# Totals of squares one half step later, and the products of w3 and w_out one step later, in a fused attention and expert kernel

## Chip, cores, metric

The kernel runs on one core of a Trainium2 chip. The metric is the device time of one execution in microseconds (us). The engines are named as in the profile: PE is TensorE (matmuls; PEld are its weight loads), DVE is VectorE, ACT is ScalarE, POOL is GpSimd, SP issues most DMAs.

## What is computed

```python
scores = np.where(mask, scale * np.matmul(q, k.transpose(0, 1, 3, 2)), -1000000000.0)
attn = softmax(scores)                 # 8 batches x 8 heads, 576 tokens, block mask of 64
x = np.matmul(attn, v)                 # put together to 4608 tokens x 512
h = (x @ w1) * (x @ w2) @ w3           # 512 -> 1024 -> 1024
x2 = h @ w_out                         # 1024 -> 512
logits = x2 @ w_gate                   # 8 experts, 576 tokens each, greedily by the largest logits
out[mask] = np.maximum(x2[mask] @ ew1[e], 0.0) @ ew2[e]
```

## The kernel before

Precise products are made from 16-bit halves: an array is scaled by a power of two, its high half is rounded to float16 by ACT (line 189), its low half is the rest, made by DVE (line 184), and a product is three matmuls (high x high, high x low, low x high). The power of two is found from a **total**: ACT squares the array and sums each row (line 203), PE sums over the 128 rows with one small matmul against a matrix of ones (`total`, line 146), and three or four short DVE instructions make the scale (`pow2`, lines 78 to 81).

The first part, up to some 700 us, interleaves three streams by an order that is written out with positions. `at(p, f)` puts a function at position p, `defer(d, f)` at d behind the present one, and functions run in the order of their positions; the unit is a **step**, about 8.5 us of PE without its extra pieces. PE issues exactly in this order. ACT, DVE and SP get their order from a scheduler that follows dependences and priorities, held by `issue_after` where `behind` is used. In step h PE does:

- the score matmuls (S, lines 330 and 394) of two tiles of rows: the second tile of half-pair h - 1 and the first of half-pair h. Eight half-pairs (steps) make one batch; group g of q and k (two head pairs of `GROUPS`) is first needed in step 8 (g // 2) + 2 (g % 2), so g = 6 in step 24, 7 in 26, 8 in 32 and so on to 15 in 58. From the fourth group on S takes the halves `qkT`: q high x k high, q high x k low, q low x k high, in this order;
- two units of the first feed-forward product (`moe_unit`, line 466, 24 matmuls each), at h + .26 and h + .60. Each takes two of the three slots of the PSUM pool `ps_ab`; ACT frees nothing before its copy `a_sb` (line 476), DVE's `g` (line 482) frees the second;
- the product of probabilities and v (PV, line 433) of an earlier half-pair, at h + .93. Behind it come ACT's and DVE's halves `xT` (lines 444 and 439).

In between ACT makes the exponentials E (line 356) and the high halves of P (line 372), DVE the maxima `nb` (line 348) and the low halves of P (line 376).

`qk_scale` prepares a group: two squares (`junk`), the total `qm`, and in `fin` two `split`s, q first, then k. A `split` asks `spread` for a place of its high half. `spread` knows two places for it in each step, .07 (behind `xT`) and .42 (behind the newest exponential, "e"); of the first two that are not before the present position and less than .75 behind it, it takes the one that fewer others have taken:

```python
PLACES = {"a": ((.07, "x"), (.42, "e")), "g": ((.3, "m"), (.58, "g")), ...
places = [x for x in places[:2] if x[0] < p + .75] or places[:1]
x, k = min(places, key=lambda x: taken_.get((key, round(x[0], 2)), 0))
```

Beside this, w_out and the eight column blocks f of w3 are read, decoded and split in the same way (`w3_chunk`, total `w3m`), and `w34` (lines 725 and 738) multiplies each block with w_out and with the gate, 24 + 16 matmuls. After the last `w34` the pool `es_g` is closed, `late_open` starts to load `g` back, and `late_run` makes the logits of eight units at a time (line 520). The second part (700 to 1024 us) multiplies with w3 w_out while DVE routes the tokens; the third does the experts.

Of the kernel before, what the change touches and what calls it, by code (L numbers as in the profile page):

```python
# [55 lines left out]
def moe_kernel(ctx, tc, q, k, v, moe_w1, moe_w2, moe_w3, moe_w_out, w_gate, ew1, ew2, out):  # L56
# [18 lines left out]
    def pow2(pool, m, name, TB=TB, **kw):  # L75
        n = m.shape[-1]
        t = pool.tile([P, 3, n], I32, name=name, **kw)
        nc.vector.tensor_scalar(t[:, 0], m.bitcast(I32), 24, 23, op0=ALU.logical_shift_right,
                                op1=ALU.logical_shift_left)
        nc.vector.tensor_scalar(t[:, 1], t[:, 0], -1.0, float((189 + TB) << 23), op0=ALU.mult, op1=ALU.add)  # L80
        nc.vector.tensor_scalar(t[:, 2], t[:, 0], float((65 - TB) << 23), None, op0=ALU.add)
        return t[:, 1].bitcast(F32), t[:, 2].bitcast(F32)
# [31 lines left out]
    ev, now, held = [], [-1.0], set()  # L114

    def at(p, f, *a):
        assert p >= now[0], (p, now[0])
        heapq.heappush(ev, (p, at.n, f, a))
        at.n += 1
# [3 lines left out]
    def defer(d, f, *a):  # L123
        at(now[0] + d, f, *a)
# [40 lines left out]
    def spread(key, p, f, *a, soon=False):  # L165
        p = max(p, now[0])
        if p < HS + .3:
            at(p, f, *a)
            return p
        if key == "a" and p > 2 * NS + 1:  # L170
            key = "t"
        places = [(x + y, k) for x in range(int(p), int(p) + 3) for y, k in PLACES[key]]
        places = [x for x in places if x[0] >= p - 1e-6]
        if soon:
            places = places[:1]
        places = [x for x in places[:2] if x[0] < p + .75] or places[:1]
        x, k = min(places, key=lambda x: taken_.get((key, round(x[0], 2)), 0))
        taken_[key, round(x, 2)] = taken_.get((key, round(x, 2)), 0) + 1
        at(x, behind, k, f, *a)
        return x  # L180

    def split(hi, lo, x, s, d=.1, p=0, then=None, key="g"):
        def low_half():
            nc.vector.scalar_tensor_tensor(lo, x, s, hi, op0=ALU.mult, op1=ALU.subtract)
            if then:
                then()

        def high_half():
            nc.scalar.activation(hi, x, AF.Copy, scale=s)
            if now[0] < HS + .3:  # L190
                defer(d, low_half)
            else:
                spread(key, now[0] + .1, low_half, soon=key != "g")

        spread("a", p, high_half, soon=key != "g")
# [5 lines left out]
    def ssq(x, dst, junk):  # L201
        with nc.allow_low_precision(reason='the sums only choose powers of two'):
            nc.scalar.activation(junk, x, AF.Square, accum_out=dst)

    def load_qk(g):
        n0, n1 = GROUPS[g]
        t = ld.tile([P, 2, 2, S], F32, name="qk32", bufs=2)
        step_ = 1 if g == 0 else 2
        for n in range(n0, n1, step_):
            for z, src in enumerate((q, k)):  # L210
                nc.sync.dma_start(t[:, z, n - n0:n - n0 + step_], src[n:n + step_].rearrange("n p s -> p n s"))
        qk32[g] = t
        if g < GF:
            for n in range(n0, n1):
                qkT[n] = t[:, 0, n - n0:n - n0 + 1], t[:, 1, n - n0:n - n0 + 1], q4f[:, n % 2:n % 2 + 1], c8
# [47 lines left out]
    pq = {}  # L263
# [3 lines left out]
    def qk_scale(g, d0, d1, d2):  # L267
        n0, n1 = GROUPS[g]
        w = n1 - n0

        def sq(z):
            if z == 0:
                pq[g] = sm.tile([P, 2], BF16, name="qm")
            ssq(qk32[g][:, z, :w], pq[g][:, z:z + 1], junk)
            if z:
                defer(d1 + (.45 if g > 5 else 0), total, pq[g], .08, fin)

        def fin(m2):
            T = c2.tile([P, 2, 2, 2, S], F16, name="qkT")
            s, e = pow2(sm, m2, "qp")  # L280
            c = sm.tile([P, 2], F32, name="cc")
            for z, f in enumerate((1.0, -1.0)):
                nc.vector.scalar_tensor_tensor(c[:, z:z + 1], e[:, 0:1], f * 0.125, e[:, 1:2],
                                               op0=ALU.mult, op1=ALU.mult)
            for z in range(2):
                split(T[:, z, 0, :w], T[:, z, 1, :w], qk32[g][:, z, :w], s[:, z:z + 1], .14,
                      then=lambda: end(d2), key="g5" if g == 4 else "g")
            pq[g] = s, c, T

        done = []  # L290

        def end(_):
            done.append(1)
            if len(done) < 2:
                return
            s, c, T = pq.pop(g)
            del qk32[g]
            for n in range(n0, n1):
                qkT[n] = T[:, 0, :, n - n0], T[:, 1, :, n - n0], q4[:, n % 2], c
            if g + 2 < len(GROUPS):  # L300
                load_qk(g + 2)

        if g == 4:
            defer(0, behind, "e", sq, 0)
            defer(.02, behind, "e", sq, 1)
            return
        spread("a", now[0], sq, 0)
        spread("a", now[0] + d0, sq, 1)

# [261 lines left out]
    def decode(key, dst, then):  # L571
        src = raw.pop(key)
        t = src.rearrange("p (n t) -> p n t", t=2)
        lo, hi = t[:, :, 0], t[:, :, 1]
        a = stg_w.tile([P, 1024], F32, name="dec2", bufs=1) if key[0] == "w" else stg.tile([P, 512], F32, name="dec", bufs=1)
        nc.scalar.activation(a, hi.bitcast(F32), AF.Abs)
        ai, d = a.bitcast(I32), dst.bitcast(I32)

        def clamp():
            nc.vector.tensor_scalar(a, a, HIMIN, HIMAX, op0=ALU.max, op1=ALU.min)  # L580
            nc.vector.tensor_scalar(ai, ai, 3, 0x3FFFFFF8, op0=ALU.logical_shift_left, op1=ALU.bitwise_and)

        def join():
            nc.vector.scalar_tensor_tensor(ai, lo, 29, ai, op0=ALU.logical_shift_right, op1=ALU.bitwise_or)
            nc.vector.scalar_tensor_tensor(d, hi, -(1 << 30), ai, op0=ALU.bitwise_and, op1=ALU.bitwise_or)
            next_load()
            defer(.05, then)

        defer(.1, clamp)
        defer(.2, join)  # L590
# [31 lines left out]
    wo = {}  # L622
# [75 lines left out]
    def w3_chunk(f, h):  # L698
        if h == 0:
            wo["w3"] = wo["p3"].tile([P, 1024], F32, name="w3d", bufs=1)  # L700
        w3 = wo["w3"]

        def use(m2):
            t = wo["T", f]
            s, e = pow2(sm, m2, "w3p")
            split(t[:, 0], t[:, 1], w3, s, .12, then=lambda: wo.update({("ok", f): True}))
            fc = sm.tile([P, 2], F32, name="w3f")
            nc.vector.tensor_tensor(out=fc[:, 0:1], in0=e, in1=wo["e"], op=ALU.mult)
            nc.vector.tensor_tensor(out=fc[:, 1:2], in0=e, in1=wo["ee"], op=ALU.mult)
            wo["T", f] = t.rearrange("p z (k f) -> p z k f", f=P), fc  # L710

        def squares():
            m = sm.tile([P, 1], BF16, name="w3m")
            wo["T", f] = wo["p3"].tile([P, 2, 1024], F16, name="w3h", bufs=2)
            at(spread("a", now[0], ssq, w3, m, wo["T", f][:, 1]) + .55, total, m, .06, use)

        decode(("3", f, h), w3[:, h * 512:h * 512 + 512], squares if h else lambda: None)

# [108 lines left out]
    for f in range(8):  # L827
        at(2 + .7 * f, prep_w, f)
        at(16.2 + .75 * f, wo_chunk, f)
        at(22.6 + .25 * f, wo_half, f)  # L830
        at(26.2 + .5 * f, wo_turn, f)
        at(29.6 + 3.2 * f, w3_chunk, f, 0)
        at(30.6 + 3.2 * f, w3_chunk, f, 1)
        at(int(33.28 + 3.2 * f) + .42, w34, f)
    at(22.2, wo_split)
    at(30.8, wo_gate)
    at(55.97, late_open)
    for h in range(UL // 8):
        at(57 + .87 * h, alone, "l", late_run, h)

    MS = {mybir.EngineType.PE}
    run(HS - .02)
# [538 lines left out]
    with tc.manual_schedule(engines={mybir.EngineType.PE, mybir.EngineType.Activation, mybir.EngineType.DVE}):  # L1381
# [3 lines left out]
        for p_ in range(E // 2):  # L1385
# [4 lines left out]
            a, b_, c = (0, 3, 6) if e == 0 else (3, 5, 8)  # L1390
# [44 lines left out]
```

## Time and profile before

| | us |
|---|---|
| median of three runs (range) | 1427.79 (1426.8 to 1428.41) |
| the profiled execution | 1425.24 |
| its span, first to last instruction | 1423.5 |
| mean granted clock of PE, share of full speed | 0.971 |
| PE busy, whole span | 1305.5 (92%) |
| DVE busy | 963.0 (68%) |
| ACT busy | 952.5 (67%) |

Busy time is time in which an engine ran an instruction; the rest is idle, and the views say what ended an idle stretch. The 1.7 us between the span and the execution's time lie around the first and last instruction.

### The profile page before, as it was taken

What the parts mean: (1) busy time and instruction counts of PE and PEld (TensorE: products, weight loads), DVE (VectorE), ACT (ScalarE), POOL (GpSimd) and SP (SyncE); (2) the same over time, 40 slices, a digit from 0 to 9 for tenths busy, and PEclk for the clock granted to TensorE, in tenths of its full rate; (3) what the DMA queues carried; (4) which work ended last, traced back from release to release, by engine and by line L of the source; (5) the groups of instructions that cost most, each with busy time, mean ns of one, the idle gap of its engine ahead of it and who ended that gap; (6) DMA issues with size and microseconds to landing.
All of it is one profiled execution on the core that took longest, in us unless ns stands there. A gap on an engine that the chain in (4) does not pass through costs nothing. (4 is left out here: it accounts for less than half of the span.)

```text
span 1423.5 us, 31849 instructions
## 1 busy us (share of the span) xinstructions
PE 1305.5 (92%) x12427; PEld 897.5 (63%) x12427; DVE 963.0 (68%) x2873; ACT 952.5 (67%) x2229; POOL 114.6 (8%) x141
## 2 busy tenths in 40 slices
PE   4669889888999989999999899999799999999997
PEld 2446567666766767666776566666586566655663
DVE  7989888887988878787415587877455456454530
ACT  7897887969888787876542555555247667675641
POOL 0000000000000000010010111101122221120001
PEclk9699999999999999999999899999989999999999
DMA  9887977797878768699999878988576677654201
GB/s 291 202 182 205 214 170 162 160 206 182 197 187 190 167 176 168 141 232 234 231 289 262 188 186 210 205 216 192 150 147 161 159 196 161 161 172 140 82 23 37
DMA packets 383814, 257.45 MB, mean 181 GB/s; under 512 B 260784, under 2 KB 344752, under 8 KB 382640
## 3 DMA queue, kind: packets, MB, share of 16 engines
q1 hardware_dynamic: 370464, 213.44, 61.6%
q0 software_dynamic: 11520, 39.87, 12.5%
q10 hardware_dynamic: 1680, 2.11, 0.5%
q8 instruction: 97, 1.59, 0.5%
q14 instruction: 53, 0.43, 0.1%
HBM read 130.84 MB, written 39.86 MB: 120 GB/s over the span
## 5 line engine op out<-in xcount | busy, mean ns | idle before, releaser
L466 PE MATMUL ab<-xT,w1h 128*128 128x288 f16 x1536 | 215.4, 289 | 12.3 <-DVE xT L439 4.0
L466 PE MATMUL ab<-xT,w2h 128*128 128x288 f16 x1536 | 212.2, 288 | 4.4 <-ACT a_sb L476 2.9
L1346 PE MATMUL pe<-xT,ewa 128*128 128x288 f16 (+2 forms) x1728 | 192.1, 274 | 1.6 <-ACT xT L1314 0.9
L466 PEld LDWEIGHTS <-w1h 128*128 128x128 f16 x1536 | 145.4, 99 | 68.8 <-issue 27.6
L1364 PE MATMUL pe<-ewb,h 128*128 128x512 f16 (+1 forms) x960 | 188.5, 379 | 0.0
L466 PEld LDWEIGHTS <-w2h 128*128 128x128 f16 x1536 | 150.8, 99 | 46.5 <-issue 6.9
L1346 PEld LDWEIGHTS <-ewa 128*128 128x128 f16 x1728 | 157.0, 99 | 36.3 <-issue 2.0
L376 DVE SCALAR_TENSOR_TENSOR P<-E,rr,P 128x128 f16<-128x128 f32 (+4 forms) x288 | 157.4, 584 | 23.7 <-ACT P L372 23.2
L356 ACT ACTIVATE E<-S,nb,cc 128x384 f32<-128x384 f32 (+4 forms) x234 | 148.0, 642 | 1.9
L1364 PEld LDWEIGHTS <-h 128*128 128x128 f16 (+1 forms) x960 | 84.7, 100 | 99.8 <-issue 2.6
L372 ACT ACTIVATE P<-E,rr 128x384 f16<-128x384 f32 (+2 forms) x224 | 120.7, 605 | 16.3 <-DVE rr L361 5.7
L1155 PE MATMUL px<-W34h,gl 128*128 128x512 f32 x288 | 120.1, 417 | 3.3 <-DMA gl<-g 3.3
L1155 PE MATMUL px<-W34h,gh 128*128 128x512 f32 x288 | 120.6, 419 | 2.3 <-ACT gh L1176 2.3
L1155 PE MATMUL px<-W34l,gh 128*128 128x512 f32 x288 | 120.0, 417 | 0.0
L433 PE MATMUL PV<-PT,v 128*64 128x128 f16 (+1 forms) x2880 | 89.9, 219 | 20.9 <-DMA PT<-P 19.7
L433 PEld LDWEIGHTS <-v 128*64 128x64 f16 x2880 | 79.0, 116 | 40.9 <-issue 32.2
L348 DVE TENSOR_REDUCE nb<-S 128x2 f32<-128x768 f32 (+3 forms) x128 | 100.7, 818 | 4.6 <-PE S L334 4.2
L1349 DVE SCALAR_TENSOR_TENSOR h<-pe,h 128x288 f16<-128x288 f32 (+2 forms) x144 | 57.8, 420 | 45.9 <-ACT h L1348 45.0
L1367 ACT ACTIVATE y<-pe,s 128x512 f32<-128x512 f32 x36 | 24.7, 687 | 94.8 <-PE pe L1364 59.6
L1304 DVE SCALAR_TENSOR_TENSOR x<-xg,xsc,x 128x512 f16<-128x512 f32 x36 | 27.1, 752 | 84.0 <-ACT x L1303 84.0
L1348 ACT ACTIVATE h<-pe 128x288 f16<-128x288 f32 (+2 forms) x144 | 52.6, 377 | 43.5 <-PE pe L1346 36.8
L1173 ACT ACTIVATE gl<-g 128x1024 fp32r<-128x1024 f32 x36 | 37.9, 1056 | 60.0 <-DMA g<-gd 59.9
(294 smaller groups left out, 2236.3 us busy)
## 6 DMA issues: line engine op xcount, KB each, us to landing
g<-gd SPq DMA_DIRECT2D x36, 512.0 KB, 5.3
gl<-g POOLq DMA_DIRECT2D x36, 512.0 KB, 5.6
raw<-in_moe_w_dram SPq DMA_DIRECT2D x32, 512.0 KB, 4.7
esa<-in_moe_w_dram SPq DMA_DIRECT2D x8, 2048.0 KB, 9.6
esb<-in_moe_w_dram SPq DMA_DIRECT2D x8, 2048.0 KB, 10.6
gd<-g SPq DMA_DIRECT2D x56, 288.0 KB, 3.1
g<-gd SPq DMA_DIRECT2D x14, 1152.0 KB, 6.7
v<-in_v_dram SPq DMA_DIRECT2D x8, 1280.0 KB, 6.9
```

Source lines behind the costliest of these rows:

```text
L348: newest["m"] = nc.vector.tensor_reduce(nb[:, 0, x:x + 2], ps[:, :, o:o + N], axis=AX.X, op=ALU.max)
L356: newest["e"] = nc.scalar.activation(d["e"][:, cols[x]], pf_[:, cols[x]], AF.Exp, bias=nb[:, 1, x:x + 1], scale=c[:, 0:1], accum_out=sums[ ...
L372: nc.scalar.activation(hi, d["e"][:, cols[x]], AF.Copy, scale=r[:, 1, x:x + 1])
L376: nc.vector.scalar_tensor_tensor(lo, d["e"][:, cols[x]], r[:, 1, x:x + 1], hi, op0=ALU.mult, op1=ALU.subtract)
L433: nc.tensor.matmul(ps[hh * 64:hh * 64 + 64, c0:c0 + w], vt[:, zv, hh, j, :], s, start=z == 0 and j == 0, stop=z == 2 and j == nj - 1)
L466: nc.tensor.matmul(p[:, :288], w[:, zw, cc, :], x[:, zx, cc, c0:c0 + 288], start=first, stop=cc == 3 and zw == 1)
L1155: nc.tensor.matmul(p, gh[a][:, f], W34[b][:, f], start=f == 0 and a + b == 0, stop=f == 7 and a == 1)
L1173: nc.scalar.activation(gh[1], g, AF.Copy, scale=-1.0)
L1346: nc.tensor.matmul(p[:, :n], w1[:, a, cc, f * P:(f + 1) * P], t[:, 4 * b + cc, x], start=cc == 0 and a + b == 0, stop=cc == 3 and a == 1)
L1348: nc.scalar.activation(h[:, 0, f, x], p[:, :n], AF.Relu)
L1349: nc.vector.scalar_tensor_tensor(h[:, 1, f, x], p[:, :n], 0.0, h[:, 0, f, x], op0=ALU.max, op1=ALU.subtract)
L1364: nc.tensor.matmul(p[r0:r1], h[:, a, f, k_ * P + r0:k_ * P + r1], EW[e, "b"][0][:, b, f], start=f == 0 and a + b == 0, stop=f == 7 and a == 1)
```

## The change

Three positions are moved. The total of q and k is placed .9 instead of .45 behind its usual distance for the groups from g = 6 on, the total of w3 1.0 instead of .55 behind its squares, and `w34`, `late_open` and the runs of logits stand one step later, the runs .85 instead of .87 apart.

```diff
             if z:
-                defer(d1 + (.45 if g > 5 else 0), total, pq[g], .08, fin)
+                defer(d1 + (.9 if g > 5 else 0), total, pq[g], .08, fin)
...
-            at(spread("a", now[0], ssq, w3, m, wo["T", f][:, 1]) + .55, total, m, .06, use)
+            at(spread("a", now[0], ssq, w3, m, wo["T", f][:, 1]) + 1.0, total, m, .06, use)
...
-        at(int(33.28 + 3.2 * f) + .42, w34, f)
+        at(int(34.28 + 3.2 * f) + .42, w34, f)
...
-    at(55.97, late_open)
+    at(56.97, late_open)
     for h in range(UL // 8):
-        at(57 + .87 * h, alone, "l", late_run, h)
+        at(58 + .85 * h, alone, "l", late_run, h)
```

In positions: the totals of q and k go from h + .49 (between the two units) to h + .94 (behind PV). `w34` goes from 33.42, 36.42, 39.42, 42.42, 46.42, 49.42, 52.42 and 55.42 to 34.42, 37.42, 40.42, 43.42, 47.42, 50.42, 53.42 and 56.42.

The first piece of the difference on PE, at step 22 (`qm` is the total of the seventh group, `wgxm` that of w_gate):

```order
 L466 MATMUL ab<-xT,w2h_81 128x288
 L146 LDWEIGHTS ones
-L146 MATMUL ab<-qm,ones 128x2
-L146 LDWEIGHTS ones
 L146 MATMUL ab<-wgxm,ones 128x1
 L466 LDWEIGHTS w1h_74
...
 L433 LDWEIGHTS v_2279
 L433 MATMUL PV<-PT_3495,v_2279 64x64
+L146 LDWEIGHTS ones
+L146 MATMUL ab<-qm,ones 128x2
 L330 LDWEIGHTS qkT
 L330 MATMUL S<-qkT 128x512
```

The total of the seventh group has left its place between two units and stands behind the PV matmuls, ahead of the next S.

On ACT in step 31, before; `qk_3855` is the group that S needs in step 32, `qk_4249` the next one, and L356 are the exponentials:

```order
L444 ACTIVATE xT<-PV 128x192
L189 ACTIVATE qkT<-qk_3855,qp 128x1152 x2
L203 ACTIVATE v_5204,vm<-v_122 128x1024
L203 ACTIVATE junk,qm<-qk_4249 128x1152
L354 ACTIVATE nb<-nb,cc 128x2
L354 ACTIVATE nb<-nb,cc 128x1
L476 ACTIVATE a_sb<-ab 128x288
L356 ACTIVATE E,sums<-S,nb,cc 128x512 x2
L356 ACTIVATE E,sums<-S,nb,cc 128x576
...
L203 ACTIVATE w3h,w3m<-w3d 128x1024
L203 ACTIVATE junk,qm<-qk_4249 128x1152
L189 ACTIVATE wgyh<-wg_4389,wgyp 128x8x8
```

and of the change, with the same group named `qk_3857`:

```order
L203 ACTIVATE junk,qm<-qk_4249 128x1152
L189 ACTIVATE qkT<-qk_3857,qp 128x1152
L203 ACTIVATE v_5195,vm<-v_122 128x512
L354 ACTIVATE nb<-nb,cc 128x2
L354 ACTIVATE nb<-nb,cc 128x1
L476 ACTIVATE a_sb<-ab 128x288
L356 ACTIVATE E,sums<-S,nb,cc 128x512 x2
L356 ACTIVATE E,sums<-S,nb,cc 128x576
L203 ACTIVATE v_5195,vm<-v_122 128x1024
L203 ACTIVATE w3h,w3m<-w3d 128x1024
L203 ACTIVATE junk,qm<-qk_4249 128x1152
L189 ACTIVATE qkT<-qk_3857,qp 128x1152
```

The two high halves stood together right behind `xT`. Now q's stands behind two squares, and k's behind the exponentials and three squares more; `wgyh` follows it.

On ACT in step 39, before (`qk_5373` is needed in step 40):

```order
L444 ACTIVATE xT<-PV 128x192
L189 ACTIVATE qkT<-qk_5373,qp 128x1152 x2
...
L356 ACTIVATE E,sums<-S,nb,cc 128x576
L203 ACTIVATE v_6770,vm<-v_122 128x1024
...
L203 ACTIVATE junk,qm<-qk_5823 128x1152
L730 ACTIVATE w34o<-ab,w3f 128x512
```

and of the change:

```order
L444 ACTIVATE xT<-PV 128x192
L189 ACTIVATE w3h<-w3d,w3p 128x1024
L203 ACTIVATE v_6758,vm<-v_122 128x1024
L203 ACTIVATE junk,qm<-qk_5775 128x1152
L189 ACTIVATE qkT<-qk_5373,qp 128x1152
...
L356 ACTIVATE E,sums<-S,nb,cc 128x512 x2
L356 ACTIVATE E,sums<-S,nb,cc 128x576
L203 ACTIVATE v_6758,vm<-v_122 128x1024
L203 ACTIVATE junk,qm<-qk_5775 128x1152
L189 ACTIVATE qkT<-qk_5373,qp 128x1152
```

The high half of w3 and a square have come in front of q's high half, k's stands behind the exponentials, and the copy of the `w34` product (`w34o`) has left the step together with its matmuls.

## Rows read from the trace of the kernel before

**Rows 1.** Length; busy time of PE, PEld, DVE, ACT, POOL; granted clock; DMA.

```profile
230.00:698.20 468.20, 440.28 (x5404) 316.74 (x5400) 381.78 (x976) 376.75 (x923) 5.98 (x13) 0.99 0.85 189
698.20:1023.70 325.50, 310.33 (x2410) 213.61 (x2406) 203.00 (x891) 159.59 (x290) 34.73 (x40) 0.98 0.86 215
```

**Rows 2.** Waits of PE from 230 to 700 us: total, times, longest.

```profile
PE ab L466 <- ACT a_sb L476: 5.5, 8, 1.0
...
PE ab L146 <- ACT junk L203: 3.1, 1, 3.1
PE ab L466 <- DVE g L482: 2.3, 1, 2.3
PE ab L146 <- ACT w3h L203: 1.9, 2, 1.2
```

**Rows 3.** Time line of PE in step 24: start, length, instruction, [idle before].

```profile
265.09 0.16 PE L146 MATMUL ab<-qm,ones 128*128 128x2 bf16 x1 [3.05 <-ACT junk L203]
265.38 3.04 PE L466 MATMUL ab<-xT,w1h 128*128 128x288 f16 x12
```

**Rows 4.** Busy time of the engines and granted clock of the stretch behind that wait.

```profile
265.00:268.40 3.40, 3.19 (x14) 2.02 (x14) 2.81 (x12) 2.33 (x8) 0.00 (x0) 0.50 0.83 151
```

**Rows 5.** Time line of PE in step 48.

```profile
524.20 0.16 PE L146 MATMUL ab<-qm,ones 128*128 128x2 bf16 x1 [1.31 <-ACT a_sb L476]
526.62 1.89 PE L466 MATMUL ab<-xT,w1h 128*128 128x288 f16 x12 [2.26 <-DVE g L482]
528.30 3.09 PE L466 MATMUL ab<-xT,w2h 128*128 128x288 f16 x12
```

**Rows 6.** Time line of PE in step 16, the S matmuls of a new group.

```profile
182.34 0.34 PE L330 MATMUL S<-qkT 64*128 64x384 f16 x2 [0.17 <-ACT qkT L189]
183.97 0.50 PE L330 MATMUL S<-qkT 64*128 64x384 f16 x4 [1.30 <-DVE qkT L184]
```

**Rows 7.** Time line of ACT in step 31, and one low half of DVE.

```profile
334.45 2.39 ACT L189 ACTIVATE qkT<-qk,qp 128x1152 f16<-128x1152 f32 x2
...
338.93 0.47 ACT L354 ACTIVATE nb<-nb,cc 128x2 f32<-128x2 f32 x2
...
339.59 0.77 ACT L356 ACTIVATE E<-S,nb,cc 128x512 f32<-128x512 f32 x1
...
341.91 1.06 ACT L203 ACTIVATE v<-v 128x1024 f16<-128x1024 f32 x1
...
343.99 1.17 ACT L203 ACTIVATE junk<-qk 128x1152 f16<-128x1152 f32 x1
...
345.13 0.35 ACT L189 ACTIVATE wgyh<-wg,wgyp 128x64 f16<-128x64 f32 x1
...
340.16 1.41 DVE L184 SCALAR_TENSOR_TENSOR qkT<-qk,qp,qkT 128x1152 f16<-128x1152 f32 x1
```

**Rows 8.** Time line of PE at the end of step 31 and in step 32.

```profile
344.15 0.16 PE L146 MATMUL ab<-w3m,ones 128*128 128x1 bf16 x1 [1.18 <-ACT w3h L203]
...
344.93 0.65 PE L330 MATMUL S<-qkT 64*128 64x384 f16 x6
```

**Rows 9.** Time line of PE, then of ACT, in step 39 and at step 40.

```profile
422.94 5.34 PE L725 MATMUL ab<-wo,w3h 128*128 128x512 f16 x24
...
428.53 1.63 PE L466 MATMUL ab<-xT,w1h 128*128 128x288 f16 x12
...
433.51 0.65 PE L330 MATMUL S<-qkT 64*128 64x384 f16 x6
...
419.32 2.38 ACT L189 ACTIVATE qkT<-qk,qp 128x1152 f16<-128x1152 f32 x2
...
428.58 0.61 ACT L203 ACTIVATE v<-v 128x512 f16<-128x512 f32 x1
```

**Rows 10.** Time line of ACT in step 55 and of PE at step 56.

```profile
596.31 2.39 ACT L189 ACTIVATE qkT<-qk,qp 128x1152 f16<-128x1152 f32 x2
...
611.01 0.65 PE L330 MATMUL S<-qkT 64*128 64x384 f16 x6
```

## The prediction

> **What bounds the kernel now.** I read the view by stretches first, then TensorE's waits, then the time lines around the instructions that move. From 230 to 698 us, the part that the change touches, TensorE (PE) is busy 440.28 of 468.20 us while VectorE (DVE) and ScalarE (ACT) have about 80% each; in the part behind it, to 1024 us, PE is busy 95% of the time [rows 1]. So PE sets the pace, its order is fixed by hand, and a microsecond that PE loses or wins before 698 us reaches the end whole: routing cannot start before the last logits. What can be won is PE's idle time there, and it is small: the reader should see waits of 3.1 us for one pair of squares (`junk`), 1.9 us in two waits for squares of w3, 2.3 us for `g`, and 5.5 us in eight waits for `a_sb` [rows 2].
>
> **What it removes.** Each total is one tiny matmul that PE meets in a fixed place. The total of the eighth group came before its squares: PE stood 3.05 us, and the next twelve matmuls took 3.04 us [rows 3] where such a dozen takes 1.63 [rows 9]. The granted clock in that stretch was 0.50, TensorE's lower level of 1.2 GHz instead of 2.4 [rows 4]. Wait and slow matmuls together: 3.05 + 1.4 = 4.5 us. The total of g = 13 shows the other price of the old place, between the two `moe_unit`s: totals take slots of `ps_ab` (three of them), so PE first stood 1.31 us for `a_sb` and then 2.26 us for `g`, and 24 matmuls took 1.89 + 3.09 us instead of 2 x 1.63 [rows 5], 1.7 more: 5.3 us. After PV, where the total now stands, the slots are empty and the squares have most of a half step more. The totals of w3 cost 1.9 us [rows 2], of which 1.18 in step 31 [rows 8]. Of the waits for `a_sb` I count half to totals between units, 2.8 us. Removed: 4.5 + 5.3 + 1.9 + 2.8 = 14.5 us. The lowest that can be removed is the totals' own waits, 3.05 + 1.31 + 1.9 = 6.3, if the slot waits only go to the next total there (the totals of v stay).
>
> **What it moves with it.** No instruction is added. But the total's later end changes which places `spread` offers to the two high halves. Before, it ran at h + .57: only 1.07 was within .75, and q and k both went there, right behind xT. Now it runs at h + 1.02: 1.07 and 1.42 both qualify, and the less used one is taken, so q stays at 1.07 and k goes to 1.42, which is behind the exponentials of that step. The order of ACT shows it: for the group that step 32 uses, k's high half stands behind the exponentials and three squares, last before `wgyh`. The S matmuls of step 32 read that half and then k's low half, which DVE makes from it. That such a lateness stops PE is seen in step 16: two S matmuls ran, and the next four waited 1.30 us for the low half [rows 6].
>
> The chain for step 32, with prices from that stretch of ACT [rows 7], from its first high half at 334.45: v 1.04 (two squares from 341.91 to 343.99 make 2.08), junk 1.14 (343.99 to 345.13), q's high half 1.20 (half of 2.39), the short square of v 0.61 [rows 9], `nb` and `a_sb` 0.66 (338.93 to 339.59), three exponentials 2.32 (339.59 to 341.91), v and w3h 2.08, junk 1.14, k's high half 1.20. Sum 11.39: k's high half ends at 345.84 and its low half, 1.41 more [rows 7], at 347.3. PE reached these S matmuls at 344.93, and without the 1.18 us wait it gets there at 343.75 [rows 8]. It stands 2.1 us, runs two matmuls (0.25), stands 1.2: 3.3 us. Behind it in PE's queue is everything, the units of step 32 first.
>
> Step 40 is the same with another piece: its `w34`, 5.59 us of PE from 422.94 to 428.53, was in step 39 and covered ACT; now it stands in step 40. From 419.32 the sum is w3's high half (taken as v's square, of the same shape, 1.04), v 1.04, junk 1.14, 1.20, 0.66, 2.32, 1.04, 1.14, 1.20 = 10.8: 430.1 and 431.5 for the low half. PE is there at 433.51 - 5.59 = 427.9 [rows 9]. It stands 2.2 + 1.2 = 3.4 us. Step 56 is step 40 again: from 596.31 to 607.1 and 608.5, PE at 611.01 - 5.59 = 605.4 [rows 10], 2.9 us. Step 24 has the same pattern with two halves of `wo` in the list and no move of `w34`; I give it the least of the others, 2.8. Step 48 I cost at nothing: the `w34` of f = 4 moves into step 47 and hides it with its 5.59 us; without that cover it would be 3.3. The other five groups (steps 26, 34, 42, 50, 58) have k's high half before the last of six exponentials. The trace shows no such order; the bounds are 0 and one high with one low half, 1.2 + 1.41 = 2.6 each. I take 0.9 each, 4.5, nearer to 0 because five exponentials must be run in any case before PE comes round.
>
> The four long waits will then be paid again in slow matmuls. The rows give 1.4 us behind 3.05 [rows 3] and 1.7 behind 1.31 + 2.26, which too had a little work in between [rows 5]; I take 1.5 each, 6.0. The Trainium skill, "TensorE: Matmul & The Clock Gate", section "HAM oscillation", says that a wait between bursts is followed by matmuls at half rate, and its worked case has 1.67 us of these per wait, a loss of half that. By that figure each would cost 0.8 us here, removed and added alike, and the sum below would be 1.2 us lower; the row has a stretch of 3.4 us at half clock, and the row decides.
>
> Moving `late_open` and the logits costs PE nothing by itself: the same matmuls stand one step later, their loads are as far ahead as before, and the last run of logits is still before the remaining units' logits. It does take two runs out of step 57, which is in the 0.9 for step 58.
>
> Sum: 3.3 + 3.4 + 2.9 + 2.8 + 4.5 + 6.0 = 22.9 added, 14.5 removed: **+8.4 us**. The profiled execution took 1425.24 us, 2.55 below the median of 1427.79; 1425.24 + 8.4 = 1433.6 for it, 1436 for the median. Bounds: all long waits without the slow clock, the five others at 0, give 12.4 - 14.5 = -2; the long waits and the five at 2.6 with slow clock give 12.4 + 13 + 6 - 6.3 = +25.
>
> **Rivals.** *Faster.* ACT reaches k's high half in time, because the hand-summed list overlaps more than the starts tell or PE comes later for other reasons. The point that decides is step 32: if k's low half is done by 343.8, nothing is added there, and the list of 11.39 us and the low half behind it must shrink by 3.5 together. Then only the five small waits stay: 1427.8 - 14.5 + 4.5 = 1418. For it: the removed waits are plain in the trace. Against: ACT runs that list without a gap in the trace of before, and xT, which starts it, waits for PE. *Cancelled.* The added waits come, but each is cut in two by the two matmuls and leaves the clock high: 16.9 - 14.5 = +2, 1430, or a little less where PE's later arrival lets ACT catch up. *Removed waits come back.* The slot waits move to the totals of v and w3, which now stand together between two units in steps 32, 40 and 48; only 6.3 us go: 22.9 - 6.3 = +17, 1444.
>
> **Numbers.** The forecast (both terms as summed) 0.50; removed waits come back 0.12; cancelled 0.15; faster 0.23. The likeliest alone lies between 1431 and 1443. The range for 8 in 10 reaches to both sides, 1420 to 1446, since the faster case and the last rival leave 0.1 each outside. About 0.2% (2.9 us) is what a measurement of this kernel can tell from no change: slower by more 0.62, within it 0.15, faster by more 0.23.
>
> **What would show it.** Right: PE's waits of S for `qkT` made by DVE and ACT, some 12 us in steps 24, 32, 40 and 56, with the granted clock at 0.50 behind them, no wait of a total for `junk`, and step 39 some 6 us shorter before its wait. Wrong: no wait of S for `qkT` above 1 us, or one in step 48, where I put none. A wait for `a_sb` or `g` of two microseconds behind the totals of v and w3 would mean that the slots were the trouble and are still. What would make the number wrong while the steps hold: ACT in step 23 to 26 is nearly full, so the wait taken from the eighth group's total may only change its name there, and the total of 14.5 would be 4.5 too high; and a transpose of P that comes late into a step without its `w34` is not in my sum.

## The result and the profile after

| | before | after |
|---|---|---|
| median (range), us | 1427.3 (1426.34 to 1428.41) | 1439.37 (1437.93 to 1440.46) |
| ratio to before, 95% interval | 1 | 1.009 [1.0074, 1.0107] |
| profiled execution, its span | 1425.24, 1423.5 | 1439.03, 1437.0 |
| mean granted clock of PE | 0.971 | 0.964 |

The kernel became 12.1 us slower. The first row of the changed kernel by stretches answers to the first of [rows 1] (start and end, length, busy time and instructions of PE, PEld, DVE, ACT, POOL, granted clock, DMA). One run of logits has moved behind its end, so the second row takes a stretch that holds the same work in both kernels, from the first score matmul of step 22 to the last logits:

```profile
230.00:705.05 475.05, 447.12 (x5431) 319.69 (x5429) 383.32 (x982) 377.60 (x925) 5.99 (x13) 0.97 0.83 184
242.00:765.60 523.60, 492.01 (x5868) 351.99 (x5866) 385.33 (x985) 392.39 (x950) 11.46 (x19) 0.98 0.86 193
```

and the same stretch of the kernel before:

```profile
238.50:752.40 513.90, 485.98 (x5868) 349.79 (x5866) 385.82 (x985) 392.28 (x949) 11.44 (x19) 0.99 0.86 196
```

The same 5868 matmuls take 9.7 us more. PE is busy 492.01 - 485.98 = 6.0 us longer with them, which is slow clock, and idle 31.6 instead of 27.9 us (length less busy time), 3.7 more. The two profiled executions are 13.8 us apart. The 3.5 us by which the stretch starts later are scatter: the code ahead of step 22 is the same, and among the fourteen kernels profiled here the step starts between 238.3 and 242.0, with no order by kernel. So the traces show some 10 of the 12 us.

PE's waits from 230 to 705 us in the changed kernel (total, times, longest), to be laid beside [rows 2]:

```profile
PE S L330 <- ACT qkT L189: 6.3, 4, 2.0
PE S L330 <- DVE qkT L184: 5.8, 6, 1.1
PE ab L466 <- DVE xT L439: 5.0, 3, 3.7
...
PE ab L466 <- ACT w34o L730: 2.3, 3, 1.0
PE ab L146 <- ACT a_sb L476: 1.3, 1, 1.3
PE ab L466 <- ACT a_sb L476: 1.1, 3, 0.7
PE ab L466 <- DVE g L482: 1.0, 2, 0.6
```

The totals no longer wait for `junk` or `w3h`, and `a_sb` has fallen from 5.5 to 1.1 us. In their place stand 12.1 us in which S waits for `qkT` (6.3 + 5.8). PE's time line shows where (start, length, instruction, [idle before]); the four pairs are steps 24, 32, 40 and 56:

```profile
262.28 0.34 PE L330 MATMUL S<-qkT 64*128 64x384 f16 x2 [1.32 <-ACT qkT L189]
263.73 0.50 PE L330 MATMUL S<-qkT 64*128 64x384 f16 x4 [1.12 <-DVE qkT L184]
...
345.77 0.34 PE L330 MATMUL S<-qkT 64*128 64x384 f16 x2 [2.04 <-ACT qkT L189]
347.22 0.82 PE L330 MATMUL S<-qkT 64*128 64x384 f16 x4 [1.12 <-DVE qkT L184]
...
434.29 0.34 PE L330 MATMUL S<-qkT 64*128 64x384 f16 x2 [1.46 <-ACT qkT L189]
435.74 0.82 PE L330 MATMUL S<-qkT 64*128 64x384 f16 x4 [1.11 <-DVE qkT L184]
...
611.41 0.34 PE L330 MATMUL S<-qkT 64*128 64x384 f16 x2 [1.46 <-ACT qkT L189]
612.87 0.82 PE L330 MATMUL S<-qkT 64*128 64x384 f16 x4 [1.12 <-DVE qkT L184]
```

Step 32 met its S matmuls without a wait before [rows 8], so did steps 40 and 56 [rows 9, 10]. Behind each pair the granted clock (last but two) is at its lower level, as it was behind the total of the eighth group [rows 4]:

```profile
264.60:268.00 3.40, 3.40 (x16) 2.14 (x15) 3.40 (x6) 3.30 (x7) 0.00 (x0) 0.50 0.91 294
346.60:350.00 3.40, 2.78 (x21) 1.78 (x21) 3.40 (x7) 1.76 (x4) 0.00 (x0) 0.50 0.41 127
435.30:438.70 3.40, 2.96 (x22) 1.91 (x22) 3.40 (x7) 2.50 (x6) 0.00 (x0) 0.50 0.52 134
612.80:616.20 3.40, 3.33 (x24) 2.10 (x24) 3.40 (x7) 1.58 (x5) 1.65 (x10) 0.50 0.74 93
```

Two waits were far from the forecast. One is for the last `xT` of step 58, which PE awaited 1.10 us before; the forecast had only its 0.9 for that step. The other, which it had at nothing, stands behind step 64, where the logits wait for `g`:

```profile
643.86 0.64 PE L466 MATMUL ab<-xT,w1h 128*128 128x288 f16 x2 [3.72 <-DVE xT L439]
...
744.20 1.18 PE L520 MATMUL ab<-g,W34g 128*32 128x288 f32 x16 [3.35 <-DMA g<-gd]
```

On SP's queue (start, time of issue) the load that this run of logits needs stands behind two loads of the second part (L1169) and is issued at 731.69. PE came to it 9.2 us later (744.20 - 3.35 - 731.69) and used it after 12.5:

```profile
723.14 8.45 SPq L1169 DMA_DIRECT2D g<-gd  x2
731.69 3.08 SPq L498 DMA_DIRECT2D g<-gd  x1
```

### The profile page after: what moved, and what is told of

Its sections match the earlier page's. It is cut to its first block, busy times and chain, and to the rows that moved or that the text cites. A ratio compares the mean times of both kernels' runs of the same rounds, so it can differ in the third digit from the quotient of the medians.

```text
span 1437.0 us, 31876 instructions
## 1 busy us (share of the span) xinstructions
PE 1315.1 (92%) x12427; PEld 901.1 (63%) x12427; DVE 962.9 (67%) x2873; ACT 952.7 (66%) x2229; POOL 114.9 (8%) x141
## 5 line engine op out<-in xcount | busy, mean ns | idle before, releaser
L466 PE MATMUL ab<-xT,w1h 128*128 128x288 f16 x1536 | 220.3, 294 | 9.5 <-DVE xT L439 5.0
L356 ACT ACTIVATE E<-S,nb,cc 128x384 f32<-128x384 f32 (+4 forms) x234 | 147.8, 640 | 1.8
L1190 ACT ACTIVATE jk<-px 128x512 f16<-128x512 f32 x36 | 21.4, 594 | 85.3 <-issue 61.5
```

Source lines behind the costliest of these rows:

```text
L356: newest["e"] = nc.scalar.activation(d["e"][:, cols[x]], pf_[:, cols[x]], AF.Exp, bias=nb[:, 1, x:x + 1], scale=c[:, 0:1], accum_out=sums[ ...
L466: nc.tensor.matmul(p[:, :288], w[:, zw, cc, :], x[:, zx, cc, c0:c0 + 288], start=first, stop=cc == 3 and zw == 1)
```

## Experiments

Theory: k's high half is late because of its new place, S waits for it, and that is where the loss comes from. Rivals: the moved logits and `w34` cost by themselves; or there is one lateness of ACT that PE meets once, under whichever name comes first, so that terms can neither be added nor won singly. Each measured time stands with its ratio to the kernel before and the 95% interval. The kernel before gave medians of 1426.99, 1426.12 and 1426.48 us beside the three sets of four runs.

### First set: the parts

**k_early**, the changed kernel with k's half at its old place:

```diff
-        spread("a", p, high_half, soon=key != "g")
+        spread("a", p, high_half, soon=early or key != "g")     # early=g > 5 for q and k
```

> The changed kernel, but k's high half is put to the first place that is offered (1.07, right behind xT), as it was before the change. Theory (the place of k's high half is what makes S wait): the waits of S for qkT, 12.1 us in all, go in steps 24, 32, 40 and 56, and with them the half-clock stretches behind steps 32, 40 and 56 (13.6 us, so some 6.8 us lost): 1420 to 1428 us against 1439.4. Rival one (the later total or a full ACT makes k late wherever its half stands): S still waits 9 us or more for qkT, 1436 to 1440 us. Rival two (the waits move to another reader of ACT, the exponentials or xT): S's waits go, but the time falls by less than 6 us, 1433 or more.

Measured: 1436.03 us, 1.0065 [1.0047, 1.0083]. S waits for `qkT` nowhere, but of the 12.1 us only some 3 are won (by the medians): rival two. PE now waits where the kernel before did or a little later, in step 24 for `a_sb` and in step 32 for `g`:

```profile
265.92 1.63 PE L466 MATMUL ab<-xT,w1h 128*128 128x288 f16 x12 [3.13 <-ACT a_sb L476]
...
349.50 2.49 PE L466 MATMUL ab<-xT,w1h 128*128 128x288 f16 x12 [3.25 <-DVE g L482]
```

The 3.13 us are the 3.05 of [rows 3] under a new name. It also waits where the kernel before did not: 2.81 and 3.28 us for `xT` in steps 34 and 50, 1.83 for `w3r` (the reduction that w34_only, below, brings up) in step 40, 2.95 for `xT` in step 58 and 3.51 for `g` of the logits.

**qk_only**, the kernel before with the first hunk of the change alone (.9 for .45).

> The kernel before with the totals of q and k alone moved (.9 instead of .45); w3, w34 and the logits stay. Theory: S waits for qkT in steps 24 (2.4 us), 32 (3.2) and 48 (about 3, since the w34 that covered it in the changed kernel is not in step 47), not in 40 and 56, whose w34 still stand in steps 39 and 55 (below 0.5 us each); the totals' own waits of 3.05 and 1.31 + 2.26 us are gone, no wait of the logits for g: 1424 to 1432 us against 1427.3. Rival (the whole loss comes with the totals of q and k, and the w34 are no cover): S waits in 40 and 56 too, 1435 to 1440 us.

Measured: 1429.84 us, 1.0017 [1.0006, 1.0029]. S waits in steps 24, 32 and 48 as expected, in the last two for less (1.32 + 1.12, 1.34 + 1.11, and the pair below, which the changed kernel does not have). It does not wait in 40 and 56, but for step 40 ACT also makes k's half early again, with q's in one stretch from 422.65 us, so that this alone does not prove the cover:

```profile
522.31 0.34 PE L330 MATMUL S<-qkT 64*128 64x384 f16 x2 [1.34 <-ACT qkT L189]
523.76 0.82 PE L330 MATMUL S<-qkT 64*128 64x384 f16 x4 [1.12 <-DVE qkT L184]
```

PE's idle time from step 22 to the last logits is 27.6 us as it was (27.9): the totals' waits that are gone pay for S's, and what remains is 2.5 us of slow matmuls. The totals of q and k with k's half late are not the 12 us by themselves.

**w34_only**, the kernel before with all the other hunks (totals of w3, `w34`, logits).

> The kernel before with the rest of the change alone: totals of w3, w34, late_open and the logits moved; the totals of q and k stay at .45. Theory (the moved logits cost by themselves: their last loads stand on SP behind two loads of the second part, 3.7 us, and step 58 has lost the two runs that covered DVE's late xT, 2.6 us; the totals of w3 give 1.9): PE waits for g behind step 64 and for xT in step 58, S waits for qkT less than 2 us in all: 1428 to 1434 us. Rival (as the prediction costed it, the move is free): neither wait, 1424 to 1427 us.

Measured: 1439.21 us, 1.0089 [1.0067, 1.0111]: above both ranges, and as slow as the whole change, with no S wait for `qkT` at all. The two waits that I had looked for are there (2.76 us for xT, 1.62 for g), but others as long are new. In steps 40 and 56, where `w34` now stands, PE waits for `w3r`, the reduction by which DVE frees the slot of the gate product behind `w34`:

```profile
445.76 1.49 PE L466 MATMUL ab<-xT,w1h 128*128 128x288 f16 x8 [2.29 <-DVE w3r L744]
...
623.89 1.36 PE L466 MATMUL ab<-xT,w1h 128*128 128x288 f16 x5 [2.78 <-DVE w3r L744]
```

In steps 34 and 50, which also got a `w34` from the step ahead of them, it waits 2.41 and 2.75 us for ACT's and DVE's `xT`, where the kernel before did not wait, and in step 32 1.31 + 2.69 us for slots. The two parts cost 2.9 and 12.2 us, the whole 12.1.

**runs_70**, the changed kernel with `58 + .70 * h` for the runs of logits.

> The changed kernel with the runs of logits 0.70 instead of 0.85 apart, so that all fourteen loads of g stand on SP ahead of the second part's first two. Theory: PE's wait of 3.7 us for g is gone and nothing takes its place: 1434 to 1437 us. Rival (the second part's loads, now behind, make its first products wait as long): the wait goes, the time stays, 1438 to 1441 us.

Measured: 1440.22 us, 1.0104 [1.0086, 1.0121], no gain. The last load now stands ahead of the second part's loads on SP, and PE waits for it all the same:

```profile
727.17 0.48 SPq L498 DMA_DIRECT2D g<-gd  x1
727.70 8.57 SPq L1169 DMA_DIRECT2D g<-gd  x2
...
739.62 1.18 PE L520 MATMUL ab<-g,W34g 128*32 128x288 f32 x16 [2.68 <-DMA g<-gd]
```

So the place in the queue is not the cause. Nor have the loads become slow by the change: in the kernel before the last two stood just ahead of the same two loads and just behind them, and PE used them without a wait:

```profile
715.48 0.36 SPq L498 DMA_DIRECT2D g<-gd  x1
723.25 3.52 SPq L498 DMA_DIRECT2D g<-gd  x1
...
727.97 1.18 PE L520 MATMUL ab<-g,W34g 128*32 128x288 f32 x16
735.07 1.18 PE L520 MATMUL ab<-g,W34g 128*32 128x288 f32 x16
```

They took 11.5 and 10.4 us to land, where the median of the fourteen was 6.7, and the DMA share of that stretch was 1.04 to 1.05; in the changed kernel and here it is 1.08. What differs is how far a load is ahead of PE: 12.5 and 11.8 us in the kernel before (727.97 - 715.48 and 735.07 - 723.25), 9.2 in the changed kernel and 9.8 here (739.62 - 2.68 - 727.17). The Trainium skill, "DMA: Bandwidth & Descriptors", section "Issuing engines are not separate DMA queues", says that all DMAs run on the same sixteen engines and interleave there; this run agrees, 2.68 us in spite of the earlier place.

### Second set: single pieces

**logits_only**, the kernel before with the last two hunk lines (`late_open` and the runs).

> The kernel before with late_open and the runs of logits alone one step later and .85 apart; all totals and w34 stay. Theory (the moved logits cost by themselves): PE waits 1.6 to 3.7 us for g behind step 64, as in the three kernels that have this move, and 2.8 to 3.7 us for xT in step 58 against 1.10 before, with slow matmuls behind it: 1431 to 1435 us against 1427. Rival (as the prediction costed it, free; the loss of w34_only is all w34's): 1426 to 1429 us.

Measured: 1427.92 us, 1.0014 [0.9999, 1.0028], in the rival's range, though both waits are there:

```profile
634.89 0.41 PE L466 MATMUL ab<-xT,w1h 128*128 128x288 f16 x2 [3.04 <-DVE xT L439]
...
740.33 1.18 PE L520 MATMUL ab<-g,W34g 128*32 128x288 f32 x16 [1.55 <-DMA g<-gd]
```

The move costs 4 us at most by the interval, and 1.8 by the medians, which is not told from nothing. The wait for xT is not the logits' alone: qk_only, whose runs of logits stand at their old places, has 3.44 us there. The size is left open; the great loss of w34_only is not here.

**after_cover**, the changed kernel with the `w34` of f = 2 and 7 back in steps 39 and 55.

```diff
-        at(int(34.28 + 3.2 * f) + .42, w34, f)
+        at(int(34.28 + 3.2 * f) + (-.58 if f in (2, 7) else .42), w34, f)
```

> The changed kernel with two of its eight w34 (f = 2 and 7) put back to steps 39 and 55, from which the change took them. Theory (these 5.6 us of PE are the cover of ACT's longest lists): the S waits of 2.57 us in steps 40 and 56 and the slow matmuls behind them (together 4.9 more than before in each) go: 1430 to 1435 us against 1439.4. Rival (ACT is late for the next reader anyway): S waits for nothing in 40 and 56, but as much is lost there to a_sb, xT or w3r, 1437 to 1440 us.

Measured: 1431.15 us, 1.0032 [1.002, 1.0044]; two of eight pieces give back 7 of the 12 us. k's half stands as late in ACT's order as in the changed kernel, but the S matmuls of step 40 that read it run without a wait:

```profile
436.47 0.65 PE L330 MATMUL S<-qkT 64*128 64x384 f16 x6
```

**k_late**, the kernel before with k's half sent to the second place, nothing else moved.

```diff
+        if late:                       # late=z and g > 5 for q and k
+            places = places[1:2]
```

> The kernel before with k's high half alone put to the second place (1.42, behind the exponentials), all totals, w34 and logits as before. The prediction's sum (added waits and the totals' waits are separate terms): S waits of 2.4 to 3.2 us in steps 24, 32 and 48 come on top of the totals' 3.05 and 1.31 + 2.26: 1434 to 1440 us against 1427. Rival (both are one lateness of ACT, which PE meets once; an S wait ahead of a total's wait takes as much from it): the total of the eighth group waits less than 1 us, 1428 to 1432 us.

Measured: 1437.19 us, 1.0071 [1.0053, 1.009]. The time is the first theory's and the mechanism is not. S waits 0.6 us for `qkT` in all: asked for before the squares of its step, k's half comes first behind the exponentials, and the squares stand behind it. What waits is then what reads the squares and what stands behind them, here in steps 31 and 32 (lines are 3 higher in this kernel):

```profile
343.21 0.16 PE L146 MATMUL ab<-w3m,ones 128*128 128x1 bf16 x1 [1.79 <-ACT w3h L206]
...
351.89 1.36 PE L469 MATMUL ab<-xT,w1h 128*128 128x288 f16 x5 [3.41 <-DVE g L485]
```

The total of step 31 had 1.18 us [rows 8]. In step 24 the total of the eighth group waits 3.13 us, for `a_sb`, not less than 1 as the rival wanted. The profiled execution took 1432.72 us, 4.5 below its kernel's median, so its trace shows only part of the loss: 7.0 us from step 22 to the last logits (520.9 against 513.9).

**qk_early**, qk_only with k's half at the old place.

> The kernel before with the totals of q and k moved (.9) and k's high half kept at the first place, behind xT; w3, w34 and logits as before. The prediction's sum: the terms for the totals of g = 7 and 13, 4.5 + 5.3 us, are won and nothing is added: 1416 to 1421 us against 1427. Rival (one lateness of ACT): in step 24 some 3 us are waited for a_sb in place of junk, as in the kernel with k's half early; what is won is in step 48 at most: 1423 to 1428 us.

Measured: 1426.2 us, 1.0 [0.9989, 1.0011]: the rival. In step 24 PE waits 3.13 us for `a_sb`, and of the 3.57 us of waits in step 48 [rows 5] 1.77 stay, for `a_sb` too. Of the 9.8 us that I had put down for these two totals nothing is seen in the time.

### Third set: where a w34 stands

**w34_and_logits**, w34_only with the totals of w3 left at .55.

> The kernel before with w34, late_open and the logits moved; all totals, those of w3 too, stay. It splits the 12 us of w34_only, of which the logits alone are 1.8. Theory (w34 covers ACT's and DVE's long lists; without it steps 34, 40, 50 and 56 lose 3 to 4.5 us each, and step 48, which gets one, wins 4.6): steps 40 and 56 wait for w3r or a_sb as in w34_only, step 32 loses 2.8 us as before, not 7.3: 1432 to 1437 us. Rival (the totals of w3 cost it, by standing with those of v and k in one step): 1427 to 1430 us.

Measured: 1437.05 us, 1.0071 [1.0055, 1.0087], above the theory's range by a hair. Steps 40 and 56 wait 2.95 and 2.90 us for `w3r`. The totals of w3 are worth 1.7 us of w34_only's loss by the medians, which the intervals do not tell from nothing; without their move the waits for `xT` in steps 34 and 50 are 0 and 0.36 us. Against logits_only the eight `w34` cost 8 to 9 us (1.0071 - 1.0014 of 1426.5 is 8.1, the medians give 9.1).

**f2_later**, the kernel before with one `w34` moved from step 39 to 40, and **f4_later**, with one moved from 46 to 47.

```diff
-        at(int(33.28 + 3.2 * f) + .42, w34, f)
+        at(int(33.28 + 3.2 * f) + (1.42 if f == 2 else .42), w34, f)     # f == 4 in f4_later
```

> The kernel before with a single move: the w34 of f = 2 goes from step 39 to step 40. Theory (cover): step 40, which lost 0.8 us in waits and slow matmuls before, loses 3.5 to 5, and nothing is won in step 39: 1429 to 1432 us against 1426.5. Rival (where a w34 stands is free): step 40 loses less than 1.5, 1426 to 1428 us.

Measured: 1429.87 us, 1.0024 [1.001, 1.0038]. S waits for no `qkT`. The wait is behind `w34` in its new step:

```profile
432.19 5.34 PE L725 MATMUL ab<-wo,w3h 128*128 128x512 f16 x24
437.37 0.55 PE L738 MATMUL ab<-wgyh,w3h 128*128 128x16 f16 x16
437.78 0.16 PE L146 MATMUL ab<-qm,ones 128*128 128x2 bf16 x1
440.90 1.63 PE L466 MATMUL ab<-xT,w1h 128*128 128x288 f16 x12 [2.96 <-DVE w3r L744]
```

`w34`, the gate product and the total hold the three slots of `ps_ab`, and in the first step of a batch DVE and ACT have six exponentials with their halves of P ahead of the copies. DVE frees the first slot here:

```profile
439.40 0.17 DVE L360 TENSOR_SCALAR rr<-sums 128x4 f32<-128x4 f32 x1 [2.15 <-ACT E L356]
...
440.68 0.17 DVE L744 TENSOR_REDUCE w3r<-ab 128x8 f32<-128x16 f32 x1
```

That is 2.8 us behind the last gate matmul (437.37 + 0.55), and DVE was idle for over half of that time: it stood 2.15 us for ACT's exponentials, and `w3r`, which reads only the slot, came behind the instructions that needed them. In step 39 `w3r` came 0.7 us behind the last gate matmul (428.12 + 0.55 to 429.34). So the sign and the time were as the theory had them, but it is the slot at the new place that costs, not a cover lost at the old one.

> The kernel before with a single move: the w34 of f = 4 goes from step 46 to step 47. Theory (cover, the other sign): ACT has 5.6 us more before the totals of step 47 and 48, whose waits (0.67, 1.31 and 2.26 us) and slow matmuls made 6.6 us before; 3 to 4.5 of it go: 1422 to 1425 us against 1426.5. Rival (the slots of the totals, not lateness, made these waits): they stay, 1426 to 1428 us.

Measured: 1423.39 us, 0.9974 [0.9961, 0.9988], faster than both kernels. The total that stood 1.31 us and let the unit wait 2.26 [rows 5] does not wait and the unit waits 0.46 (time line of PE in step 48):

```profile
522.60 0.17 PE L146 MATMUL ab<-qm,ones 128*128 128x2 bf16 x1
523.23 1.02 PE L466 MATMUL ab<-xT,w1h 128*128 128x288 f16 x7 [0.46 <-ACT a_sb L476]
```

The window around it, with the columns of the stretches above, has the clock at 1.00:

```profile
518.00:526.00 8.00, 7.54 (x79) 5.65 (x74) 6.87 (x23) 7.01 (x21) 0.00 (x0) 1.00 0.99 198
```

and in the kernel before:

```profile
524.00:532.00 8.00, 5.54 (x49) 3.70 (x50) 7.33 (x25) 7.93 (x23) 0.00 (x0) 0.79 0.60 141
```

Here the cover is shown: 5.6 us of PE ahead of ACT's list, where nothing of `w34` is in the way. In step 49 1.08 us are lost to `w3r`.

**mix**, qk_only with k's half early for the group of step 32 and f4_later's move.

> The kernel before with what won in the runs: totals of q and k at .9 (3.2 to 4 us won in steps 24 to 31), k's high half of the group of step 32 kept at the first place (3 us of qk_only's loss there), the w34 of f = 4 in step 47 (3 to 4 us). w3 totals, the other w34 and the logits as before. Theory (the losses of single steps add up): 1421 to 1425 us. Rival (each step's loss only moves to the next reader of ACT): 1426 to 1429 us.

Measured: 1423.52 us, 0.9985 [0.9973, 0.9998]: in the theory's range, but no better than f4_later alone, and qk_early won nothing with the totals either. PE waits 3.72 us for xT in step 58, as it waits 3.44 in qk_only.

## Why the prediction was right, and where its steps were not

The forecast was 1436, slower, with 1431 to 1443 as the likeliest case's own range; 1439.37 lies in it. The sum held better than its parts. Its idle time was forecast 5.6 us up (16.9 of S's waits less 3.05 + 3.57 + 1.9 + 2.8 of the old ones) and rose by 3.7; its slow matmuls were forecast at 2.9 and came to 6.0.

- **Removed, 14.5.** The waits named went from the trace: `a_sb`, `junk`, `w3h`, `g` fell from 12.8 us in [rows 2] to 2.1. But qk_early shows that they are not a saving on their own: without S's waits nothing of the time is won. The risk that I named for the eighth group's total, that its wait only changes its name, is what happens, 3.13 us for `a_sb` in place of 3.05.
- **Added waits of S.** Steps 24, 32, 40, 56: 2.44, 3.16, 2.57, 2.58 us against 2.8, 3.3, 3.4, 2.9; step 48 none, as forecast; two of the five others (26 and 34) 0.81 and 0.54, the rest none that the trace shows, against 0.9 each. 12.1 us in all for 16.9.
- **Slow clock.** The net term was 6.0 - 3.1 = +2.9 and PE's busy time rose by 6.0: 6.8 us of half clock stand behind the wait of step 32 (346.6 to 353.4), and 3.4 more behind xT in step 58. How much of it another execution of the same kernel would show is open (last section). The Trainium skill, "TensorE: Matmul & The Clock Gate", section "HAM oscillation", has 1.67 us at half clock per wait in its worked case, of which it counts half, 0.8 us, as lost; by that the net term would be an estimate of 1.6, and the trace went the other way.
- **The step that failed: the moved `w34` and logits, costed at nothing.** That "their loads are as far ahead as before" was wrong: PE came 9.2 us behind the issue of a load instead of 11.8 to 12.5, in a stretch where loads took 10.4 to 11.5 us in the kernel before already, and waits 3.35 us for it. The wait for step 58's xT became 3.72 instead of 1.10, but either move makes it (3.04 in logits_only, 3.44 in qk_only). In time the logits' move is 1.8 us, hardly told from nothing. The greater omission was `w34` itself. I had it only as cover for k's halves; in its new steps 40 and 56 it also takes slots that DVE and ACT free late. The moved `w34` alone, with k's half early, cost 8 to 9 us, with 5.9 us of waits for `w3r` in these two steps; what the other six pieces cost was not split, but for f = 4, which by itself wins 3.
- **The step that failed: terms added.** The parts cost 2.9 and 12.2 and the whole 12.1; k's half put back gives 3, two `w34` put back give 7. In the changed kernel S's wait in step 40 comes first and takes the place of the wait for `w3r`. The prediction put on k's half what the moved `w34` costs without it too. The time came out because one wait took the other's place; to that extent the number was luck.

Open stay the exact price of the logits' move, why k_late is 11 us slower when its trace shows 7 of it, and the 5 us that remain in after_cover: S still waits there in steps 24 and 32 (2.43 and 3.16 us), but what these two waits are worth was not tried by itself.

## What to carry to other kernels

When an engine is nearly full over a step, a wait of PE for it can behave like a debt of that step: here moving the reader mostly changed the wait's name (k_early, qk_early), while work of PE put ahead of it won time (f4_later). The order of the other engines is a second handle: k_late moved one kind of instruction on ACT and lost 11 us, and in f2_later DVE had `w3r` behind instructions that waited. A row that shows a wait does not show its cause: the load for the logits was about as slow in the kernel before, only further ahead of PE. Before moving a matmul piece to another step, count the PSUM slots it holds and look how soon the engines that free them come round in the new step; one such piece won 3 us by a move of one step and another lost 3. Try such moves one at a time: here the others hid the one that was worth keeping.

## What the runs showed of the hardware that was not expected

A wait's length alone did not decide whether slow matmuls followed. Behind 1.46 + 1.11 us in step 40 of the changed kernel the granted clock was 0.50; behind a single wait of 3.13 us in k_early and of 2.96 in f2_later it stayed at 1.00 (the first row is k_early's, the second f2_later's):

```profile
265.90:269.30 3.40, 3.38 (x34) 2.53 (x35) 3.34 (x13) 3.37 (x11) 0.00 (x0) 1.00 0.91 177
```

```profile
440.90:444.30 3.40, 3.40 (x39) 2.71 (x40) 2.86 (x12) 2.15 (x6) 0.00 (x0) 1.00 1.18 124
```

Ahead of f2_later's wait stood the dense 24 matmuls of `w34`, ahead of step 40's S wait the PV matmuls. That alone cannot be the difference. In f2_later, whose order is that of the kernel before up to step 39, the total of the eighth group comes before its squares behind the same two dozens of matmuls and waits as long as in [rows 3]; but there the clock stays at 1.00, and the dozen behind it takes 1.63 us instead of 3.04:

```profile
266.80 0.16 PE L146 MATMUL ab<-qm,ones 128*128 128x2 bf16 x1 [3.06 <-ACT junk L203]
267.09 1.63 PE L466 MATMUL ab<-xT,w1h 128*128 128x288 f16 x12
```

```profile
266.80:270.20 3.40, 3.27 (x28) 2.51 (x29) 2.72 (x12) 3.37 (x11) 0.00 (x0) 1.00 0.77 141
```

So slow matmuls behind a wait, such as the 1.4 us behind the 3.05, are partly a matter of the single execution; what decides it was not tried.
